# Banded attention and a routed expert layer: values as the stationary operand in column halves, and the output kept transposed

## The chip, the cores and the metric

The kernel runs on one core of one Trainium2 chip. The metric is the device time of one execution in microseconds; the median of several runs is compared. All data are 32-bit floats.

## What is computed

Attention over 4 batches, 8 heads, 768 positions and head dimension 64, in which a query sees the 8 first keys and its last 96 keys, with a bias that grows with the distance; its output is the input `x` (3072 x 512) of a layer of 8 experts, where each token goes to its one best expert.

```python
scores = scale * np.matmul(q, k.transpose(0, 1, 3, 2))
keep = is_global | is_local                 # first 8 keys, or 0 <= rel < 96
scores = np.where(keep, scores + bias, -1e9)
a = np.exp(scores - scores.max(-1)); a = a / (a.sum(-1) + 1e-9)
x = (a @ v).transpose(0, 2, 1, 3).reshape(3072, 512)
logits = x @ w_gate                         # 512 x 8
e = argmax(logits); gate = softmax(logits)[e]
out = gate * (relu(x @ w1[e]) @ w2[e])      # w1 512 x 1024, w2 1024 x 512 for each expert
```

## The kernel before

**Attention** (`banded_attention`, from L322). The work is cut into 48 units: batch b, pair of heads j (4 of them), and block c of 256 queries (3 of them). Queries are taken in tiles of 128. A tile needs two blocks of 128 keys: its own, and a block `kA` (values: `va`) that holds the keys of the tile before with the first 16 replaced by the first 16 of the sequence. So a unit has 4 blocks, the first of a sequence (c = 0) 3.

A unit n goes through these steps:

- `scores` (L447): PE multiplies keys by queries for each block and head, the two heads in the two halves of the rows (L458, 64x128 tiles). The result has keys in the partitions and queries along the free axis. ACT takes the exponential from PSUM (L461), DVE multiplies by a table `W` of exp(-bias) with zeros where nothing is kept (L467 for c = 0, L472 once for each head otherwise).
- `attend` (L478): PE multiplies with the exponentials as the stationary operand, 128x128, and the values as the moving one (L490). The values stand in the tile with a column of ones behind each block of 64, so the sum of each query's weights comes out as a column of its own. The output has queries in the partitions. DVE takes the reciprocal of the four sums of each query (L494, 128x4) and scales the output with it into `xr` (L497).
- `turn` (L501): PE turns `xr` by the identity (L506), ACT copies it to `xl` (L509). After the last pair of heads, the queue of SP stores `xr` to `x_tok` in DRAM, one token's 2 KB in each partition (L231).
- `logits` (L513) and `logits_sum` (L527), only in the last pair: the gate's product, in four column tiles of 32 (L521), and the sum of its four parts (L534). `gate`, `spread` and `spread_sum` then count and place the tokens of a batch, mostly small DVE operations.

The program is in the order that the loop at L718 writes out; each engine runs its instructions in that order. In iteration n stand: `scores(n)`, `turn(n-4)`, `logits(n-5)`, `attend(n-2)`, `logits_sum(n-5)`; for c = 0 `turn_qk` of the next pair (DVE turns its keys and queries, L409 and L410, and POOL makes `kA`, L374 and L376); for c = 1 `turn_v` (POOL makes `va`, L400 and L401). SP's queue loads q, k and v two and three pairs ahead, and from unit 8 to 43 expert 0's weights, one transfer in two of three units (L715, L716).

**After the last unit** expert 0's first 256 tokens are computed in pieces (`work`, L640: L293 and L300) between the steps of the last batch's routing. POOL gathers tokens from `x_tok` by indirect DMA, 32 tokens at a time (L256), and DVE turns them into columns (L263). The layout of a token in `x_tok`, of `turn_x` and of w1's rows hang together: before, w1 is loaded with its rows permuted to fit.

**Experts** (from L972). For each of the seven others, in order of size: the hidden layer (L1007, ACT's Relu L1009), then the result (L1033 or L1025), scaling and scatter. While one expert runs, SP loads the next one's w1 (L236, four transfers of 512 KB by groups of 32 partitions) and w2 (L992, one of 2 MB).

A check at the end (`ground`, L961) tests that all reciprocals lie in a range; if not, a general path runs, which it does not for this input.

Of the kernel before, what the change touches and what calls it, by code (L numbers as in the profile page):

```python
# [24 lines left out]
R_MIN = 2.0 ** -100  # L25
R_MAX = 2.0 ** 60
# [3 lines left out]
def kernel(  # L30
# [28 lines left out]
    x_tok = nc.dram_tensor("x_tok", (N * NJ, P), F32)  # L59

    w1v = moe_w1.rearrange("e (j k q) f -> j q e k f", j=NJ, q=32)
# [34 lines left out]
    vts = [consts.tile([P, 2 * NB * (D + 1) + P - D - 1], F32, name=f"vt{i}") for i in range(3)]  # L96

    def ones_in(t):
        w = 2 * NB * (D + 1)
        nc.gpsimd.memset(t[:, 0:w].rearrange("p (c w) -> p c w", w=D + 1)[:, :, D:D + 1], 1.0)  # L100
        nc.gpsimd.memset(t[:, w:], 1.0)

    ones_in(vts[0])
# [79 lines left out]
    recips = consts.tile([P, 2 * B * H * NB // 4, 2], F32)  # L183
# [44 lines left out]
    def store(t0, n, xr):  # L228

        for i in range(n):  # L230
            nc.sync.dma_start(x_tok[NJ * (t0 + P * i):NJ * (t0 + P * i + P), :].rearrange("(p j) d -> p (j d)", j=NJ),  # L231
                              xr[:, i, :])

    def expert_w1(to, e):
        for j in range(NJ):
            nc.sync.dma_start(to[32 * j:32 * j + 32, :, :, :], w1v[j, :, e, :, :])  # L236
# [10 lines left out]
    def rows_of(ps, nm, ns, mw, to_rows):  # L247

        pw = ps.tile([P, NS * TB], F32, tag="m", name="pw" + nm)[:, 0:TB * ns]
        nc.tensor.matmul(pw, lhsT=sel, rhs=mw.rearrange("p s g -> p (s g)"), start=True, stop=True)  # L250
        nc.vector.tensor_scalar(out=to_rows, in0=pw, scalar1=float(NJ), scalar2=j_of[:, 0:1], op0=ALU.mult, op1=ALU.add)

    def gather(xq, cols, n, top=N):

        for i in range(n):
            nc.gpsimd.indirect_dma_start(out=xq[:, i, :], out_offset=None, in_=x_tok[0:NJ * top, :],  # L256
                                         in_offset=bass.IndirectOffsetOnAxis(ap=cols[:, i:i + 1], axis=0),
                                         bounds_check=NJ * top - 1, oob_is_err=False)
# [63 lines left out]
    def banded_attention():  # L322
        with ExitStack() as actx:
            mp = actx.enter_context(tc.tile_pool(name="maskb", bufs=1))
            xlp = actx.enter_context(tc.tile_pool(name="xlb", bufs=3))
            xrp = actx.enter_context(tc.tile_pool(name="xrb", bufs=5))
# [10 lines left out]
            VW = D + 1  # L337
            NV = 3
            VT, VA = NB * VW, (NB - 1) * VW
            vas = [vp.tile([P, 2 * VA + P - VW], F32, name=f"va{i}") for i in range(2)]  # L340
            for i, t in enumerate(vts):
                if i > 0:
                    ones_in(t)
            for t in vas:
                nc.gpsimd.memset(t[:, 2 * VA:], 1.0)
# [17 lines left out]
            def load_v(pr):  # L363
                b, j = divmod(pr, NJ)
                vt = vts[pr % NV]
                for h in range(2):
                    (nc.scalar if pr == 0 and h == 0 else nc.sync).dma_start(
                        vt[:, VT * h:VT * h + VT].rearrange("p (c w) -> p c w", w=VW)[:, :, 0:D],
                        v[b, 2 * j + h].rearrange("(c p) d -> p c d", p=P))
# [3 lines left out]
            def keys_at(kT, kA, a0, a1):  # L373
                nc.gpsimd.tensor_copy(out=kA[:, a0:a1, GW:P],  # L374
                                      in_=kT[:, a0 * P:a1 * P].rearrange("p (c t) -> p c t", t=P)[:, :, GW:P])
                nc.gpsimd.tensor_copy(out=kA[:, a0:a1, 0:GW],  # L376
# [18 lines left out]
            def turn_v(pr):  # L395
                vt = vts[pr % NV]
                va = vas[pr % 2]
                to = va[:, 0:2 * VA].rearrange("p (h x) -> p h x", h=2)
                vh = vt[:, 0:2 * VT].rearrange("p (h x) -> p h x", h=2)
                nc.gpsimd.tensor_copy(out=to, in_=vh[:, :, 0:VA])  # L400
                nc.gpsimd.tensor_copy(  # L401
                    out=to[0:GW, :, VW:VA].rearrange("p h (c w) -> p h c w", w=VW),
                    in_=vh[0:GW, :, 0:VW].rearrange("p h (o w) -> p h o w", o=1).to_broadcast([GW, 2, NB - 2, VW]))
                pairs[pr] += [vt, va]

            def turn_qk(pr):
# [4 lines left out]
                keys_at(kT, kA, 0, NB - 1)  # L411
# [29 lines left out]
            xrs = {}  # L441
# [5 lines left out]
            def scores(n):  # L447
                b, j, c = units[n]
                qT, kT, kA, _, _ = pairs[b * NJ + j]
# [11 lines left out]
                nc.scalar.activation(e[:, :, 0:w], ps[:, :, 0:w], AF.Exp, scale=D ** -0.5)  # L461
                if n == 0:
                    turn_first(2, NB, ps_s.tile([P, 2, 512], F32, tag="s", name="first_1"))
                elif c == 1 and b == 0 and j + 1 < NJ:
# [4 lines left out]
                else:  # L469
                    for h in range(2):  # L470
                        eh = e[:, h, :].rearrange("p (t c) -> p t c", t=2)
                        nc.vector.tensor_tensor(  # L472
                            out=eh, in0=eh,
                            in1=W[:, 2 * j + h, P:3 * P].rearrange("p (o c) -> p o c", o=1).to_broadcast([P, 2, 2 * P]),
                            op=ALU.mult)
                st[n] = e

            def attend(n):  # L478
                b, j, c = units[n]
                _, _, _, vt, va = pairs[b * NJ + j]  # L480
# [3 lines left out]
                for t in range(2):  # L484
                    mine = [(m, own) for m, (u, own) in enumerate(bl) if u == t]
                    for h in range(2):
                        for m, own in mine:
                            i = 2 * c + t
                            c0 = VT * h + VW * i if own else VA * h + VW * (i - 1)
                            nc.tensor.matmul(po[:, t, h, :], lhsT=pt[:, h, P * m:P * m + P],  # L490
                                             rhs=(vt if own else va)[:, c0:c0 + P],
                                             start=(m == mine[0][0]), stop=(m == mine[-1][0]))
                r = recips[:, 2 * n:2 * n + 2, :]
                nc.vector.reciprocal(r.rearrange("p t (h o) -> p t h o", o=1), po[:, :, :, D:D + 1])  # L494
                if j == 0:
                    xrs[b, c] = xrp.tile([P, 2, DM], F32, tag="xr", name=f"xr_{b}_{c}")
                nc.vector.tensor_tensor(  # L497
                    out=xrs[b, c][:, :, P * j:P * j + P].rearrange("p t (h d) -> p t h d", h=2), in0=po[:, :, :, 0:D],
                    in1=r.rearrange("p t (h o) -> p t h o", o=1).to_broadcast([P, 2, 2, D]), op=ALU.mult)

            def turn(n):  # L501
                b, j, c = units[n]
                xr = xrs[b, c]
                px = ps_m.tile([P, 2, P], F32, tag="m", name=f"px_{n}")
                for t in range(2):
                    nc.tensor.transpose(px[:, t, :], xr[:, t, P * j:P * j + P], ident)  # L506
                if j == 0:
                    xls[b, c] = xlp.tile([P, KC, 2 * P], F32, tag="xl", name=f"xl_{b}_{c}")
                nc.scalar.copy(out=xls[b, c][:, j, :], in_=px.rearrange("p t c -> p (t c)"))  # L509
                if j == NJ - 1:  # L510
                    store(S * b + 2 * P * c, 2, xrs.pop((b, c)))
# [199 lines left out]
            turn_v(0)  # L711
# [3 lines left out]
            weights_0 = [lambda f0=f0: nc.sync.dma_start(w2_0[:, :, f0:f0 + 1, :], w2v[:, 0:1, f0:f0 + 1, :]) for f0 in range(FC)]  # L715
# [422 lines left out]
```

## Time and profile before

| | us |
|---|---|
| median of 3 runs | 604.67 (602.85 to 605.37) |
| the profiled execution | 607.0 |
| its span, first to last instruction | 605.1 |
| PE busy | 547.9 (91%) |
| DVE busy | 199.1 (33%) |
| ACT busy | 101.8 (17%) |
| POOL busy | 179.7 (30%) |

PE is the matrix engine, PEld its weight loads, DVE the vector engine, ACT the scalar engine, POOL the general one, SP the one that issues most DMAs. A 32-bit matmul has two records in the profile, a turn by the identity one; records of PE overlap, so the price of one is read from the starts of a series. A wait is put down to what ended it, and "issue" means that nothing recorded ended it. By stages: the attention runs to 185 us, the last batch's routing with expert 0 to 284 us, the other experts to the end.

### The profile page before, as it was taken

How to read it: one execution, taken by the hardware profiler on the slowest of the kernel's cores; microseconds unless marked ns; L12 is line 12 of the kernel's file. 1: busy time of each engine (PE TensorE's matmuls, PEld its weight loads, DVE VectorE, ACT ScalarE, POOL GpSimd, SP SyncE). 2: the span in 40 equal slices, each digit the busy share in tenths (PEclk: the TensorE clock that was granted, in tenths of full speed). 3: DMA queues.
4: the chain of work that ended last, by engine and by line, in shares of the span. 5: the costliest groups of instructions: out<-in, count | busy, mean ns of one | idle time of the engine just before them, and what ended most of it. 6: DMA issues, size and time to landing. Idle time of an engine off the chain costs nothing.

```text
span 605.1 us, 7929 instructions
## 1 busy us (share of the span) xinstructions
PE 547.9 (91%) x3034; PEld 379.4 (63%) x3034; DVE 199.1 (33%) x526; ACT 101.8 (17%) x193; POOL 179.7 (30%) x228
## 2 busy tenths in 40 slices
PE   4999999999998991199999999999999969999994
PEld 3998888998886851184555555555555747554541
DVE  3877876967851633002001301300301301200000
ACT  2543333333232100010110110110110110100100
POOL 4332224222250177601700730620550450101001
PEclk9999999999998996579999999999999998999999
DMA  9999999989212085107561534642625626401000
GB/s 154 147 166 160 235 175 171 217 132 234 64 55 86 5 204 194 50 7 179 167 139 43 185 81 89 214 97 58 205 59 117 202 48 131 176 1 50 1 18 36
DMA packets 145232, 71.96 MB, mean 119 GB/s; under 512 B 126743, under 2 KB 126747, under 8 KB 145184
## 3 DMA queue, kind: packets, MB, share of 16 engines
q1 hardware_dynamic: 137344, 58.16, 45.9%
q0 software_dynamic: 5312, 12.59, 6.5%
q10 hardware_dynamic: 2528, 0.59, 0.6%
q8 instruction: 26, 0.43, 0.3%
q14 instruction: 22, 0.18, 0.1%
HBM read 59.07 MB, written 12.91 MB: 119 GB/s over the span
## 4 chain that ended last, share of the span: by engine, by line
PE 85%; issue 5%; DVE 4%; DMA 2%; another core or an unknown queue 1%; POOL 1%; SPq 0%; ACT 0%; ACTq 0%; POOLq 0%; DVEq 0%
PE ph L1007 24%; PE po L1033 17%; PE o L490 12%; PE s L458 7%; PE po L1025 7%; PE ph L293 6%; PE po L300 4%; PE px L506 3%; PE pt L1042 1%; PE pq L521 1%; PE pi L598 1%; DMA vt<-in_v_dram 1%; DVE y L282 1%; DMA qb<-in_q_dram 1%
## 5 line engine op out<-in xcount | busy, mean ns | idle before, releaser
L256 POOL DMA_INDIRECT xq_s<-x_tok,rows_s x85 | 85.4, 1004 | 25.9 <-issue 24.4
L274 POOL DMA_INDIRECT out_dram<-y,idx_s x25 | 24.3, 973 | 211.2 <-DVE y L282 208.4
L1007 PE MATMUL ph<-xe,w_second 128*128 128x416 f32 (+2 forms) x256 | 81.9, 479 | 0.0
L1009 ACT ACTIVATE hT<-ph 128x416 f32<-128x416 f32 (+2 forms) x56 | 27.7, 495 | 278.2 <-PE ph L1007 233.5
L490 PE MATMUL o<-vt,e 128*128 128x128 f32 x384 | 72.8, 278 | 0.0
L1035 DVE COPY yT<-po 128x416 f32<-128x416 f32 (+1 forms) x20 | 11.3, 565 | 183.8 <-PE po L1033 183.8
L1007 PEld LDWEIGHTS ph<-xe,w_second 128*128 128x128 f32 x256 | 48.4, 190 | 31.9 <-issue 20.5
L1033 PE MATMUL po<-hT,w_second 128*128 128x416 f32 (+1 forms) x192 | 63.8, 493 | 5.1 <-ACT hT L1009 5.1
L1007 PE MATMUL ph<-xe,w_first 128*128 128x416 f32 (+1 forms) x192 | 66.3, 503 | 0.0
L293 PE MATMUL ph<-xe,w_first 128*128 128x128 f32 x256 | 38.2, 304 | 30.0 <-issue 27.2
L490 PE MATMUL o<-va,e 128*128 128x128 f32 x320 | 62.8, 278 | 0.0
L461 ACT ACTIVATE e<-s 128x1024 f32<-128x1024 f32 (+1 forms) x48 | 45.7, 953 | 95.9 <-PE s L458 48.1
L490 PEld LDWEIGHTS o<-vt,e 128*128 128x128 f32 x384 | 57.6, 194 | 1.6 <-issue 1.2
L1033 PEld LDWEIGHTS po<-hT,w_second 128*128 128x128 f32 x192 | 38.0, 199 | 30.4 <-issue 20.4
L293 PEld LDWEIGHTS ph<-xe,w_first 128*128 128x128 f32 x256 | 35.5, 217 | 32.8 <-issue 29.9
L1007 PEld LDWEIGHTS ph<-xe,w_first 128*128 128x128 f32 x192 | 36.2, 190 | 27.8 <-issue 19.7
L472 DVE TENSOR_TENSOR e<-e,Wb 128x512 f32<-128x512 f32 x64 | 44.4, 736 | 18.7 <-ACT e L461 16.3
L490 PEld LDWEIGHTS o<-va,e 128*128 128x128 f32 x320 | 48.7, 193 | 2.6 <-issue 2.5
L1033 PE MATMUL po<-hT,w_first 128*128 128x416 f32 x128 | 45.0, 512 | 0.0
L458 PE MATMUL s<-qT,kT 64*128 64x128 f32 x384 | 40.6, 290 | 0.9 <-ACT qT L392 0.9
L458 PE MATMUL s<-qT,kA 64*128 64x128 f32 x320 | 35.7, 301 | 2.9 <-POOL kA L376 2.9
L1033 PEld LDWEIGHTS po<-hT,w_first 128*128 128x128 f32 x128 | 24.3, 190 | 20.4 <-issue 20.1
(167 smaller groups left out, 525.0 us busy)
## 6 DMA issues: line engine op xcount, KB each, us to landing
w_second<-in_moe_w_dram SPq DMA_DIRECT2D x16, 512.0 KB, 9.5
w_second<-in_moe_w_dram SPq DMA_DIRECT2D x4, 2048.0 KB
x_tok<-xr SPq DMA_DIRECT2D x24, 256.0 KB, 4.0
w_first<-in_moe_w_dram SPq DMA_DIRECT2D x12, 512.0 KB, 7.8
w_first<-in_moe_w_dram SPq DMA_DIRECT2D x3, 2048.0 KB
vt<-in_v_dram SPq DMA_DIRECT2D x31, 192.0 KB, 4.7
qb<-in_q_dram SPq DMA_DIRECT2D x60, 96.0 KB, 4.1
kb<-in_k_dram SPq DMA_DIRECT2D x60, 96.0 KB, 3.8
```

The costliest lines, as they stand in the source:

```text
L256: nc.gpsimd.indirect_dma_start(out=xq[:, i, :], out_offset=None, in_=x_tok[0:NJ * top, :], in_offset=bass.IndirectOffsetOnAxis(ap=cols[:, ...
L274: p = nc.gpsimd.indirect_dma_start(out=out[:, :], out_offset=bass.IndirectOffsetOnAxis(ap=where, axis=0), in_=y[0:rows, :], in_offset=None ...
L293: nc.tensor.matmul(ph[:, P * f:P * f + P], lhsT=w1_0[:, 0, kc, c0:c0 + P], rhs=xe_0[q % 2][:, kc, :], start=(kc == 0), stop=(kc == KC - 1))
L300: nc.tensor.matmul(po, lhsT=hT_0[q % 2][:, fc, :], rhs=w2_0[:, 0, fc, :], start=(fc == 0), stop=(fc == FC - 1))
L458: nc.tensor.matmul(ps[:, h, P * m:P * m + P], lhsT=lhsT, rhs=qT[r, P * i:P * i + P], start=True, stop=True)
L461: nc.scalar.activation(e[:, :, 0:w], ps[:, :, 0:w], AF.Exp, scale=D ** -0.5)
L472: nc.vector.tensor_tensor(out=eh, in0=eh, in1=W[:, 2 * j + h, P:3 * P].rearrange("p (o c) -> p o c", o=1).to_broadcast([P, 2, 2 * P]), op= ...
L490: nc.tensor.matmul(po[:, t, h, :], lhsT=pt[:, h, P * m:P * m + P], rhs=(vt if own else va)[:, c0:c0 + P], start=(m == mine[0][0]), stop=(m ...
L1007: nc.tensor.matmul(ph[:, 0:C], lhsT=w1t[:, 0, kc, P * fc:P * fc + P], rhs=xe[:, kc, 0:C], start=(kc == 0), stop=(kc == KC - 1))
L1009: nc.scalar.activation(hT[:, fc, 0:C], ph[:, 0:C], AF.Relu)
L1025: nc.tensor.matmul(po, lhsT=hT[:, fc, P * q:P * q + P], rhs=w2t[:, 0, fc, :], start=(fc == 0), stop=(fc == FC - 1))
L1033: nc.tensor.matmul(po[:, 0:C], lhsT=w2t[:, 0, fc, P * dc:P * dc + P], rhs=hT[:, fc, 0:C], start=(fc == 0), stop=(fc == FC - 1))
```

## The change

- In `attend` the values are the stationary operand, 64 columns wide, and the exponentials the moving one. The two heads of a pair are written to the two halves of the output's partitions, head by head in turn. The output is x transposed: features in the partitions, queries along the free axis.
- The column of ones in the value tiles goes, with the memsets for it. In its place a 128x64 block of ones is multiplied by the exponentials, so that each of a head's 64 rows of the output holds the sum of every query: 4 matmuls a unit, of 256 columns each (for c = 0 two of 256 and two of 128).
- The reciprocal is now taken of that whole block (128x256), and scales the output straight into `xl`.
- `turn` on PE and its ACT copy go. DVE turns `xl` in blocks of 32x32 to `xt` for the store, which is 4 transfers of 32 partitions with pieces of 512 bytes, and stands right behind `attend(n-2)`. A token's row in `x_tok` has another order inside, so w1 is loaded with its rows in their natural order.
- The multiplication by `W` in units of 4 blocks is one instruction for both heads.
- The copies for `kA` and `va` go from POOL to ACT and one unit later.
- The check uses sums that ACT accumulates beside the exponentials (`sums`), and one more exponential for each unit that flags sums that are too small (`small`).
- Expert 0's weights are loaded in units 36 to 43, two transfers of 256 KB in each. The other experts' w1 goes in 4 transfers by blocks of rows, w2 in 4 of 512 KB.
- After the last unit `attend`, `turn` and the gate's steps stand in another order.

The diff, without the general path, the changes to sizes of pools and the check:

```diff
-    vts = [consts.tile([P, 2 * NB * (D + 1) + P - D - 1], F32, name=f"vt{i}") for i in range(3)]
+    vts = [consts.tile([P, 2, NB, D], F32, name=f"vt{i}") for i in range(3)]
...
-    def store(t0, n, xr):
-        for i in range(n):
-            nc.sync.dma_start(x_tok[NJ * (t0 + P * i):NJ * (t0 + P * i + P), :].rearrange("(p j) d -> p (j d)", j=NJ),
-                              xr[:, i, :])
+    def store(t0, n, xt):
+        rows = x_tok[TB * t0:TB * (t0 + P * n), :].rearrange("(c t a) d -> a t c d", t=32, a=TB)
+        for a in range(TB):
+            nc.sync.dma_start(rows[a], xt[32 * a:32 * a + 32, :, :])
 
     def expert_w1(to, e):
-        for j in range(NJ):
-            nc.sync.dma_start(to[32 * j:32 * j + 32, :, :, :], w1v[j, :, e, :, :])
+        for kc in range(KC):
+            nc.sync.dma_start(to[:, :, kc:kc + 1, :], w1v[:, e, kc:kc + 1, :])
+    def expert_w2(to, e):
+        for fc in range(0, FC, 2):
+            nc.sync.dma_start(to[:, :, fc:fc + 2, :], w2v[:, e, fc:fc + 2, :])
...
             def keys_at(kT, kA, a0, a1):
-                nc.gpsimd.tensor_copy(out=kA[:, a0:a1, GW:P],
+                nc.scalar.copy(out=kA[:, a0:a1, GW:P],
...
-                nc.gpsimd.tensor_copy(out=to, in_=vh[:, :, 0:VA])
+                nc.scalar.copy(out=va, in_=vt[:, :, 0:NB - 1, :])
...
-                nc.scalar.activation(e[:, :, 0:w], ps[:, :, 0:w], AF.Exp, scale=D ** -0.5)
+                nc.scalar.activation(e[:, :, 0:w], ps[:, :, 0:w], AF.Exp, scale=D ** -0.5, accum_out=sums[:, n:n + 1])
                 if n == 0:
                     turn_first(2, NB, ps_s.tile([P, 2, 512], F32, tag="s", name="first_1"))
+                    turn_v(0)
...
                 else:
-                    for h in range(2):
-                        eh = e[:, h, :].rearrange("p (t c) -> p t c", t=2)
-                        nc.vector.tensor_tensor(
-                            out=eh, in0=eh,
-                            in1=W[:, 2 * j + h, P:3 * P].rearrange("p (o c) -> p o c", o=1).to_broadcast([P, 2, 2 * P]),
-                            op=ALU.mult)
+                    eh = e.rearrange("p h (t c) -> p h t c", t=2)
+                    nc.vector.tensor_tensor(
+                        out=eh, in0=eh,
+                        in1=W[:, 2 * j:2 * j + 2, P:3 * P].rearrange("p h (o c) -> p h o c", o=1).to_broadcast([P, 2, 2, 2 * P]),
+                        op=ALU.mult)
...
-                    for h in range(2):
-                        for m, own in mine:
-                            i = 2 * c + t
-                            c0 = VT * h + VW * i if own else VA * h + VW * (i - 1)
-                            nc.tensor.matmul(po[:, t, h, :], lhsT=pt[:, h, P * m:P * m + P],
-                                             rhs=(vt if own else va)[:, c0:c0 + P],
+                    for m, own in mine:
+                        i = 2 * c + t
+                        for h in range(2):
+                            nc.tensor.matmul(po[D * h:D * h + D, 0, t, :],
+                                             lhsT=vt[:, h, i, :] if own else va[:, h, i - 1, :],
+                                             rhs=pt[:, h, P * m:P * m + P],
                                              start=(m == mine[0][0]), stop=(m == mine[-1][0]))
-                r = recips[:, 2 * n:2 * n + 2, :]
-                nc.vector.reciprocal(r.rearrange("p t (h o) -> p t h o", o=1), po[:, :, :, D:D + 1])
+                if c == 0:
+                    parts = [(pt[:, :, 0:4 * P].rearrange("p h (t c) -> p h t c", t=2)[:, :, :, 0:P], 0), (pt[:, :, P:2 * P], 1)]
+                else:
+                    both = pt.rearrange("p h (t o c) -> p h o t c", t=2, o=2)
+                    parts = [(both[:, :, o, :, :], 0) for o in range(2)]
+                for i, (e, t0) in enumerate(parts):
+                    for h in range(2):
+                        nc.tensor.matmul(po[D * h:D * h + D, 1, t0:2, :], lhsT=ones[:, 0:D], rhs=e[:, h],
+                                         start=(i == 0), stop=(i == len(parts) - 1))
+                r = rp.tile([P, 2, P], F32, tag="r", name=f"r_{n}")
+                nc.vector.reciprocal(r, po[:, 1, :, :])
...
-                nc.vector.tensor_tensor(
-                    out=xrs[b, c][:, :, P * j:P * j + P].rearrange("p t (h d) -> p t h d", h=2), in0=po[:, :, :, 0:D],
-                    in1=r.rearrange("p t (h o) -> p t h o", o=1).to_broadcast([P, 2, 2, D]), op=ALU.mult)
+                xl = xls[b, c][:, j, :]
+                nc.vector.tensor_tensor(out=xl.rearrange("p (t c) -> p t c", t=2), in0=po[:, 0, :, :], in1=r, op=ALU.mult)
+                nc.scalar.activation(junk, po[:, 1, :, :].rearrange("p t c -> p (t c)"), AF.Exp, scale=-2.0 / S_MIN,
+                                     accum_out=small[:, n:n + 1])
 
             def turn(n):
                 b, j, c = units[n]
-                xr = xrs[b, c]
-                px = ps_m.tile([P, 2, P], F32, tag="m", name=f"px_{n}")
-                for t in range(2):
-                    nc.tensor.transpose(px[:, t, :], xr[:, t, P * j:P * j + P], ident)
-                if j == 0:
-                    xls[b, c] = xlp.tile([P, KC, 2 * P], F32, tag="xl", name=f"xl_{b}_{c}")
-                nc.scalar.copy(out=xls[b, c][:, j, :], in_=px.rearrange("p t c -> p (t c)"))
+                nc.vector.transpose(xts[b, c][:, :, j, :], xls[b, c][:, j, :].rearrange("p (c t) -> p c t", t=32))
...
-                    if n % 3 > 0 and 8 <= n < 44:
+                    if 36 <= n < 44:
+                        weights_0.pop(0)()
                         weights_0.pop(0)()
...
                 if 0 <= n - 4 < nu:
-                    turn(n - 4)
-                if 0 <= n - 5 < nu:
-                    logits(n - 5)
+                    logits(n - 4)
                 if 0 <= n - 2 < nu:
                     attend(n - 2)
+                    turn(n - 2)
...
                 if n < nu and c == 1 and pr + 1 < B * NJ:
+                    keys_at(*pairs[pr + 1][1:3], 0, NB - 1)
+                if n < nu and c == 2 and pr + 1 < B * NJ:
                     turn_v(pr + 1)
...
-            turn_x(xe_0[0], xq_0[0], TB)
-            turn(nu - 3)
             attend(nu - 1)
-            turn_x(xe_0[1], xq_0[1], TB)
-            work(2)
-            turn(nu - 2)
-            logits(nu - 3)
             turn(nu - 1)
-            work(1)
+            logits(nu - 3)
+            turn_x(xe_0[0], xq_0[0], TB)
+            turn_x(xe_0[1], xq_0[1], TB)
             logits(nu - 2)
+            work(2)
             logits(nu - 1)
-            work(1)
+            work(2)
```

## The prediction

> **What bounds the kernel now.** I read the sums by stage first, because the page's average mixes an attention part with an expert part. Columns: stretch, its length, then busy time (and instructions) of PE, weight loads, DVE, ACT, POOL, the granted clock, DMA share, GB/s.
>
> ```profile
> 50.00:100.00 50.00, 49.02 (x506) 43.71 (x506) 38.43 (x87) 18.48 (x33) 13.03 (x20) 1.00 1.03 189
> 100.00:150.00 50.00, 49.28 (x512) 43.48 (x511) 37.36 (x86) 18.43 (x34) 13.04 (x21) 1.00 0.99 190
> ...
> 220.00:240.00 20.00, 8.67 (x48) 6.73 (x47) 7.19 (x25) 0.00 (x0) 15.35 (x16) 0.75 0.77 223
> 240.00:260.00 20.00, 4.01 (x11) 2.83 (x11) 0.00 (x0) 0.00 (x0) 12.01 (x12) 0.50 0.16 43
> ...
> 320.00:420.00 100.00, 99.18 (x305) 54.77 (x304) 16.01 (x43) 8.27 (x16) 29.88 (x30) 1.00 0.43 115
> ```
>
> In the attention PE has no idle time, and DVE, at 77%, has little to spare. The DMA engines are as full as PE, but PE doesn't wait for them. The experts are PE alone. Between lies a hole (220 to 260), which the timeline of PE explains in part:
>
> ```profile
> 222.58 4.07 PE L293 MATMUL ph<-xe,w_first 128*128 128x128 f32 x35
> ...
> 243.66 0.37 PE L293 MATMUL ph<-xe,w_first 128*128 128x128 f32 x1 [2.43 <-issue]
> ...
> 259.06 11.69 PE L293 MATMUL ph<-xe,w_first 128*128 128x128 f32 x79 [0.82 <-issue]
> ```
>
> From 226.6 to 259.1 PE gets one matmul in about 2.4 us and waits for nothing that is recorded. Its 16 matmuls need 2 us; some 31 us are lost in issue.
>
> Then one attention unit in the timeline of PE (start, length, what):
>
> ```profile
> 103.50 0.51 PE L534 MATMUL pl<-sel,lq 128*128 128x8 f32 x4
> 103.94 0.49 PE L458 MATMUL s<-qT,kA 64*128 64x128 f32 x4
> ...
> 105.03 0.44 PE L506 MATMUL px<-ident,xr 128*128 128x128 f32 x2
> 105.40 0.64 PE L521 MATMUL pq<-xl,wg_sb 128*32 128x256 f32 x8
> 105.97 0.49 PE L490 MATMUL o<-va,e 128*128 128x128 f32 x2
> ```
>
> Starts give the price. Scores take 1.09 us for 8 matmuls (two records each), since two halves of the rows run at once; the values (105.97 to 107.86) 1.89 for 8, or 0.22 each; the turn 0.37. The gate's L521 uses quarters of the columns: four matmuls of 256 columns in 0.57 us, where 0.22 for 128 columns would make 1.8 one after another. Column tiles do overlap here.
>
> Last, the groups of DVE by shape (busy, mean ns, idle before):
>
> ```profile
> L497 DVE TENSOR_TENSOR xr<-o,recips 128x256 f32<-128x256 f32 x44 | 18.7, 424 | 1.5
> L467 DVE TENSOR_TENSOR e<-e,Wb 128x768 f32<-128x768 f32 x14 | 13.5, 964 | 7.3 <-ACT e L461 7.3
> L409 DVE STREAM_TRANSPOSE kT<-kb 128x768 f32<-128x768 f32 x13 | 12.6, 968 | 0.0
> L494 DVE RECIPROCAL recips<-o 128x4 f32<-128x4 f32 x44 | 7.8, 177 | 12.8 <-PE o L490 12.6
> L263 DVE STREAM_TRANSPOSE xe<-xq 128x128 f32<-128x128 f32 x16 | 4.0, 288 | 3.2 <-DMA xq<-x_tok,rows 2.8 <-issue 0.3
> L537 DVE COPY L<-pl 128x16 f32<-128x16 f32 x12 | 2.0, 167 | 11.5 <-PE pl L534 11.5
> L224 DVE RECIPROCAL gates<-se 128x6 f32<-128x6 f32 x4 | 0.8, 191 | 0.1
> ```
>
> [...] This trace shows it only with 4 and 6 elements, 177 and 191 ns: 7 ns for an element more, where an ordinary operation adds about 1 (768 against 256 elements: 540 ns for 512). [...]
>
> **The change part by part.** All of the attention is counted for a pair of heads (three units, one with 3 blocks and two with 4), 16 pairs in all. Before, the first reciprocal starts at 20.8 and the last at 184.5: 163.7 us, 10.2 a pair.
>
> PE. Removed: three turns, 1.1 us. The values become 128x64 tiles, two heads side by side: 22 matmuls of 0.22 (4.9) become 11 pairs (2.45). Added: sums, in pairs, of 256+128, 512 and 512 columns at 0.22 per 128: 2.2 to 2.45. Scores stay at 3.05 (0.87 + 2 x 1.09), routing at about 1.45 (four matmul groups of L521 and after, 5.8 a batch). PE goes from 10.5 to about 9.6 with 0.2 for switching tiles: 0.9 a pair less.
>
> DVE. An independent successor starts 0.08 before an operation's recorded end (kT at 104.33 for 0.97, qT at 105.23), a dependent one 0.03 after it.
> - Multiplications: 768 elements 0.88; the 1024 of a 4-block unit, now in one instruction, 0.96 + 256 x 1.04 ns - 0.08 = 1.15. Sum 3.2.
> - Reciprocal: from 128x4 to 128x256, because the block of ones gives every row of the output its sum. The trace doesn't show this size. [...] like L497: 0.42. [...] I take the line through the two rows: fixed part 149 ns (L537 leaves 150 after its 16 elements), 256 x 7 ns: 1.94. Three with the dependent start: 5.9.
> - Scaling stays 0.42, now with the transpose dependent on it: 1.35 for three.
> - New transposes of 256 elements: between L263 (0.288) and L409 (0.968), 0.43 less the overlap, 0.35: 1.05.
> - kT and qT: 0.89 + 0.86 = 1.75.
>
> Sum 13.2 a pair; 16 pairs less one qk: 210. Three batches' routing lies among it at about 5.7 each (the fourth batch's: 1.6 for the gate from 198.0, the rest to 204.2): 17. So 227 us of DVE against 9.6 x 16 = 154 of PE: VectorE becomes the bound, and PE's saving is worth nothing. DVE's first multiplication starts at 11.0; with some 2.5 us of filling the last unit ends near 240.5, where it ended at 185.1: +55.
>
> ACT. Per pair: exponentials 2.9; the check of small sums, three of 256 from PSUM like L509 (0.37), 1.1; the copies for kA and va, which POOL did in 970, 745, 655 and 251 ns, about 2.2 from ACT's own slope of 0.83 ns an element; less L509's 1.1. The accumulations are not in the trace: 0 to 0.2 each, 1.2 at most. Sum 6.2 to 7.4, hidden behind 13.2 of DVE. A copy for kA waits for kT, and the next exponential stands behind it in ACT's queue; the exponential has over 3 us of slack a unit, so nothing. Without that cover it would cost 2 us a pair.
>
> POOL loses its copies and memsets: nothing, it was idle four fifths of the time.
>
> DMA and SP. Expert 0's 4 MB go out in units 36 to 43, two issues a unit. They have 8 x 4.7 = 38 us; at the 190 GB/s shown they need 21, and they are first read after the last unit: hidden. Each is an issue on SP ahead of later q, k and v loads, 0.3 us like L236's: nothing. Freeing the early DMA gains nothing, since PE doesn't wait there. Stores go from 24 to 48 of half the size, w2 from one issue to four, all off the path: PE is 99% busy in the experts.
>
> End of the attention: the first turn_x now stands behind a transpose more, three turns on PE are gone: 0 within 1 us. The experts are unchanged.
>
> Sum: span 605.1 + 55 = 660. The profiled execution took 607.0, 2.3 above the median of 604.67; a difference carries over, so **660 us**.
>
> **Rivals.**
> B, the same, but the issue hole goes: nothing that I can name fixes its place. For it: 288 more records (576 instructions) go through PE before it[...]. Against: the weights and gathers around it are the same. 660 - 31 = 629.
> C, column halves with 128 rows don't overlap: PE takes 3.05 + 4.9 + 4.9 + 1.45 = 14.3 a pair, 229 us, beside DVE's 227. Both full, about 10 more: 670. Against it: L521.
> D, faster: [...] the 14 ns between its two rows are something else. DVE then needs 8.7 + 1.1 a pair, PE 9.6: PE stays the bound and wins 0.9 x 16 = 14: 591. It decides at the length at which DVE fills the old 10.2 a pair: (10.2 - 8.4) / 3 = 0.6 us for one reciprocal.
> E, the hole moves or grows, or the gain and loss cancel: within 0.5% by chance.
>
> **How the numbers follow.** Forecast 0.52, B 0.28, C 0.07, D 0.10, E 0.03. [...] So 622 (B's low end) to 680 [...] leaves D and little else out. Faster by over 0.5% (what a measurement here can tell from no change) 0.11, within 0.02, slower 0.87.
>
> **What would show it.** Right: a reciprocal group 128x256 near 1.9 us, x48; DVE over 95% busy from 50 to 230 and PE near two thirds; the L490 row's successor at about 0.22 us a pair of heads; ACT's waits for scores or free tiles. Wrong: a reciprocal near 0.4; PE still full in the attention; the issue hole absent, which alone moves the time by 31.

## The result and the profile after

| | before | after |
|---|---|---|
| median | 605.0 us (4 runs, 602.9 to 608.9) | 715.5 us (4 runs, 711.1 to 715.8) |
| ratio | | 1.180, 95% interval 1.174 to 1.187 |
| span of the profiled execution | 605.1 | 709.4 |
| last scaling of the attention ends | 185.1 | 292.6 |

The change makes the kernel slower by 110 us; the forecast was 55. All of the excess is in the attention, which ends 107.5 us later in the profiles. From there to the end the two spans agree to 3 us (420.0 and 416.8).

The sums by stage, after the change (stretch, length, then busy us and instructions of PE, weight loads, DVE, ACT and POOL, clock, DMA share, GB/s):

```profile
50.00:100.00 50.00, 37.56 (x372) 27.64 (x372) 37.28 (x44) 19.30 (x51) 0.00 (x0) 0.80 0.50 101
100.00:150.00 50.00, 35.39 (x342) 27.85 (x344) 37.42 (x59) 17.38 (x45) 0.00 (x0) 0.76 0.42 79
```

In the forecast VectorE stood at over 95% here. It stands at 75%, as before the change (76%); PE falls from 98% to 73%, and ACT has 37%. No engine is full, so the engines must be waiting for each other, and the groups of instructions say for whom (busy us, mean ns of one, idle us before them and what ended it):

```profile
L492 DVE RECIPROCAL r<-o 128x256 f32<-128x256 f32 x48 | 83.9, 1748 | 0.4 <-PE o L489 0.3
L460 DVE TENSOR_TENSOR e<-e,Wb 128x1024 f32<-128x1024 f32 x32 | 38.8, 1212 | 26.5 <-ACT e L449 25.3
L446 PE MATMUL s<-qT,kA 64*128 64x128 f32 x320 | 43.3, 355 | 46.7 <-ACT kA L368 46.6
L498 ACT ACTIVATE junk<-o 128x256 f32<-128x256 f32 x48 | 18.4, 384 | 174.6 <-DVE xl L497 172.5
L449 ACT ACTIVATE e<-s 128x1024 f32<-128x1024 f32 x32 | 32.6, 1019 | 1.2 <-PE s L446 1.1
```

PE waits for ACT, DVE waits for ACT, and ACT waits 172.5 us for DVE at one instruction: L498, the exponential that flags sums that are too small ("the check" from here on). PE itself hardly holds anybody up: the exponentials L449 wait 1.1 us for it in all, the reciprocals L492 0.3. Here is one unit of 4 blocks, first in ACT's timeline, then in DVE's (start, length, what, idle before):

```profile
51.41 1.02 ACT L449 ACTIVATE e<-s 128x1024 f32<-128x1024 f32 x1
52.32 0.20 ACT L449 ACTIVATION_READ_ACCUMULATOR e<-s 128x1 f32 x1
56.02 0.38 ACT L498 ACTIVATE junk<-o 128x256 f32<-128x256 f32 x1 [3.50 <-DVE xl L497]
...
56.39 0.71 ACT L390 COPY va<-vt 128x640 f32<-128x640 f32 x1
57.14 0.62 ACT L391 COPY va<-vt 16x512 f32<-16x512 f32 x1
57.66 0.80 ACT L449 ACTIVATE e<-s 128x768 f32<-128x768 f32 x1
```

```profile
52.55 1.22 DVE L460 TENSOR_TENSOR e<-e,Wb 128x1024 f32<-128x1024 f32 x1 [1.86 <-ACT e L449]
53.70 1.75 DVE L492 RECIPROCAL r<-o 128x256 f32<-128x256 f32 x1
55.48 0.42 DVE L497 TENSOR_TENSOR xl<-o,r 128x256 f32<-128x256 f32 x1
...
58.58 0.96 DVE L456 TENSOR_TENSOR e<-e,Wb 128x768 f32<-128x768 f32 x1 [2.20 <-ACT e L449]
```

Read by turns, the two timelines are one chain:

1. The exponential of unit n starts at 51.41 on ACT, and its multiplication at 52.55 on DVE.
2. Behind that, in DVE's order, stand the reciprocal and the scaling of unit n-2 (53.70 and 55.48).
3. The check of unit n-2 waits for the scaling and starts at 56.02 on ACT.
4. Behind the check, in ACT's order, stand the copies and then the exponential of unit n+1, at 57.66. With it the chain begins again.

The check reads only the sums, which PE had written before the reciprocal of 53.70 began to read them. But the sums lie in the same PSUM tile as the products that the scaling reads. In the program as built the check waits for PE and for the scaling on VectorE, because the text has it behind the scaling. The two only read that tile, and they share nothing else.

One pair (three units) without routing, from the starts between 51.41 and 68.30, in us:

| unit | exponential to multiplication | to reciprocal | to scaling | to check | to next exponential | sum |
|---|---|---|---|---|---|---|
| 4 blocks, `va` copies behind the check | 1.14 | 1.15 | 1.78 | 0.54 | 1.64 | 6.25 |
| 3 blocks | 0.92 | 0.88 | 1.78 | 0.52 | 0.38 | 4.48 |
| 4 blocks, keys and queries turned ahead, `kA` copies | 1.65 | 1.10 | 1.78 | 0.55 | 1.08 | 6.16 |

That is 16.9 us a pair. VectorE's own work is 12.6 a pair, as the first experiment shows, and the kernel before took 9.1 (from one pair's first multiplication to the next one's, in pairs without routing).

### The profile page after: what moved, and what is told of

It reads as the page before. It is cut to its first block, busy times and chain, and to the rows that moved or that the text cites. A ratio compares the mean times of both kernels' runs of the same rounds, so it can differ in the third digit from the quotient of the medians.

```text
span 709.4 us, 8708 instructions
## 1 busy us (share of the span) xinstructions
PE 577.2 (81%) x3322; PEld 378.0 (53%) x3322; DVE 285.8 (40%) x542; ACT 142.5 (20%) x355; POOL 136.6 (19%) x154
## 4 chain that ended last, share of the span: by engine, by line
PE 56%; DVE 25%; ACT 9%; issue 6%; SPq 2%; DMA 1%; another core or an unknown queue 1%; DVEq 0%; ACTq 0%; POOL 0%; POOLq 0%
PE ph L1005 21%; PE po L1031 15%; DVE r L492 10%; PE po L1023 6%; PE ph L291 5%; DVE e L460 4%; PE po L298 4%; ACT e L449 4%; DVE xl L497 3%; DVE e L456 2%; DVE kT L398 2%; DVE qT L399 2%; PE pi L592 1%; PE s L446 1%; ACT va L390 1%
## 5 line engine op out<-in xcount | busy, mean ns | idle before, releaser
L492 DVE RECIPROCAL r<-o 128x256 f32<-128x256 f32 x48 | 83.9, 1748 | 0.4 <-PE o L489 0.3
L446 PE MATMUL s<-qT,kA 64*128 64x128 f32 x320 | 43.3, 355 | 46.7 <-ACT kA L368 46.6
L254 POOL DMA_INDIRECT xq<-x_tok,rows x16 | 16.5, 1032 | 301.1 <-DVE early L615 271.0
L446 PEld LDWEIGHTS s<-qT,kA 64*128 64x128 f32 x320 | 30.3, 231 | 58.3 <-ACT kA L368 49.1
L291 PE MATMUL ph<-xe,w_first 128*128 128x128 f32 x256 | 35.5, 289 | 30.0 <-issue 26.9
L489 PE MATMUL o<-e,ones 128*64 128x256 f32 (+1 forms) x384 | 57.5, 429 | 0.0
L478 PE MATMUL o<-e,vt 128*64 128x128 f32 x384 | 45.8, 324 | 9.9 <-ACT junk L498 9.9
L498 ACT ACTIVATE junk<-o 128x256 f32<-128x256 f32 x48 | 18.4, 384 | 174.6 <-DVE xl L497 172.5
L460 DVE TENSOR_TENSOR e<-e,Wb 128x1024 f32<-128x1024 f32 x32 | 38.8, 1212 | 26.5 <-ACT e L449 25.3
L446 PE MATMUL s<-qT,kT 64*128 64x128 f32 x384 | 45.3, 318 | 2.2 <-DVE qT L399 1.1
L449 ACT ACTIVATE e<-s 128x1024 f32<-128x1024 f32 (+1 forms) x48 | 45.3, 944 | 1.2 <-PE s L446 1.1
```

The costliest lines, as they stand in the source:

```text
L291: nc.tensor.matmul(ph[:, P * f:P * f + P], lhsT=w1_0[:, 0, kc, c0:c0 + P], rhs=xe_0[q % 2][:, kc, :], start=(kc == 0), stop=(kc == KC - 1))
L446: nc.tensor.matmul(ps[:, h, P * m:P * m + P], lhsT=lhsT, rhs=qT[r, P * i:P * i + P], start=True, stop=True)
L460: nc.vector.tensor_tensor(out=eh, in0=eh, in1=W[:, 2 * j:2 * j + 2, P:3 * P].rearrange("p h (o c) -> p h o c", o=1).to_broadcast([P, 2, 2, ...
L478: nc.tensor.matmul(po[D * h:D * h + D, 0, t, :], lhsT=vt[:, h, i, :] if own else va[:, h, i - 1, :], rhs=pt[:, h, P * m:P * m + P], start= ...
L489: nc.tensor.matmul(po[D * h:D * h + D, 1, t0:2, :], lhsT=ones[:, 0:D], rhs=e[:, h], start=(i == 0), stop=(i == len(parts) - 1))
L492: nc.vector.reciprocal(r, po[:, 1, :, :])
```

## The experiments

Theory L: this loop of ACT's and VectorE's queues, closed by the check's wait, sets the pace. Its rivals are:

- C: the copies that came to ACT hold PE's scores up (46.6 us of waits for `kA`).
- K: PE's half clock after its gaps (granted clock 0.50 from 68.45 to 74.20 after the change, 1.00 from 50 to 150 before it) is a cause by itself.
- S: the check's own time counts.
- V: VectorE's own sum sets the pace, which was the forecast.

Chips turned out to differ, so an excess below ("+55.0") is over the kernel before on the same chip. The +110.4 of the change is from the runs of the result, over 605.0; the first chip's excesses are over 608.0. A difference of the two can be off by these 3 us, so the end of the attention (of its last scaling) in the profiles is the closer measure.

**Check ahead of the reciprocal** (first chip)

```diff
+                nc.scalar.activation(junk, po[:, 1, :, :].rearrange("p t c -> p (t c)"), AF.Exp, scale=-2.0 / S_MIN,
+                                     accum_out=small[:, n:n + 1])
                 nc.vector.reciprocal(r, po[:, 1, :, :])
...
-                nc.scalar.activation(junk, po[:, 1, :, :].rearrange("p t c -> p (t c)"), AF.Exp, scale=-2.0 / S_MIN,
-                                     accum_out=small[:, n:n + 1])
```

> The check exponential stands ahead of the reciprocal instead of behind the scaling; nothing is left out. Theory L (a loop of the two queues): in the kernel after the change, exponential n, multiplication n, reciprocal n-2, scaling n-2, check n-2, copies, exponential n+1 follow one another, 4.5 + 5.7 + 6.2 = 16.4 us a pair by the starts in the timeline. With the check ahead, ACT waits for PE alone, the reciprocals lie beside the next exponential, and VectorE's own sum of 12.8 a pair is left (3.2 multiplications, 5.35 reciprocals, 1.4 scaling, 1.1 transposes, 1.75 keys and queries): 16 pairs and 17 of routing end near 234 instead of 293, so about 655. Rival C (the copies for kA and va on ACT hold PE's scores up): the copies are as before, so within 10 of 715. Rival K (TensorE's half clock by itself): no change, 715. Rival S (the check's own time on ACT counts): no change, 715.

Measured: 663.0 us against 608.0, ratio 1.094 (1.087 to 1.100): +55.0 where the change has +110.4. The attention ends at 240.3 instead of 292.6. One statement in another place gives 52 us back (55 by the excesses). By stages:

```profile
50.00:100.00 50.00, 38.62 (x409) 29.32 (x405) 48.15 (x73) 21.10 (x56) 0.00 (x0) 0.86 0.60 118
100.00:150.00 50.00, 41.38 (x451) 31.25 (x451) 45.21 (x62) 23.71 (x61) 0.00 (x0) 0.88 0.59 116
```

VectorE is at 93% now. In pairs without routing its operations stand one behind the other, with no wait left:

```profile
54.77 1.18 DVE L460 TENSOR_TENSOR e<-e,Wb 128x1024 f32<-128x1024 f32 x1
55.87 1.75 DVE L494 RECIPROCAL r<-o 128x256 f32<-128x256 f32 x1
57.65 0.42 DVE L499 TENSOR_TENSOR xl<-o,r 128x256 f32<-128x256 f32 x1
58.11 0.45 DVE L503 STREAM_TRANSPOSE xt<-xl 128x256 f32<-128x256 f32 x1
58.48 1.18 DVE L460 TENSOR_TENSOR e<-e,Wb 128x1024 f32<-128x1024 f32 x1
```

ACT now runs ahead of VectorE. The exponential of 54.75 belongs to the multiplication of 58.48, and the check of 55.75 to the reciprocal of 59.59, 3.8 us later; the next unit's exponential (57.38) runs before either:

```profile
54.75 1.01 ACT L449 ACTIVATE e<-s 128x1024 f32<-128x1024 f32 x1
...
55.75 0.37 ACT L492 ACTIVATE junk<-o 128x256 f32<-128x256 f32 x1
...
57.38 0.80 ACT L449 ACTIVATE e<-s 128x768 f32<-128x768 f32 x1
```

Pairs without routing take 12.6 us, VectorE's sum. Theory L had said 655; the rest is mostly routing, which took 23 us where 17 were counted. The copies were as in the change, and PE's clock was still below full (0.86 to 0.88, after 0.76 to 0.80), so C and K fall as the main cause. V does not explain the change itself, where VectorE stood at 75%; it holds here.

In the program as built the reciprocal now waits for the check, the other way round. Where the check comes late, the trace has this wait:

```profile
106.53 1.76 DVE L494 RECIPROCAL r<-o 128x256 f32<-128x256 f32 x1 [0.95 <-ACT junk L492]
```

So the order of the two readers follows the text. That it hangs on the shared tile is read from the program; a tile of its own for the sums was not tried.

**Check left out** (first chip)

```diff
+    nc.gpsimd.memset(small, 0.0)
...
-                nc.scalar.activation(junk, po[:, 1, :, :].rearrange("p t c -> p (t c)"), AF.Exp, scale=-2.0 / S_MIN,
-                                     accum_out=small[:, n:n + 1])
```

> The check exponential is left out (its 48 flags are set to 0 once): the small sums are not looked for, the rest is computed. Theory L: as with the check ahead, within 3 us of that kernel, near 655, since ACT's time is not on the path once it does not wait for VectorE. Rival S (the check's own time counts, 48 x 0.57 = 27): 27 less than the kernel with the check ahead. Rival C: 715 less at most 27.

This kernel does not look for small sums. Measured: 663.7, ratio 1.093 (1.087 to 1.099), the same as with the check ahead. So 48 exponentials of 0.38 us and 48 readings of the accumulator of 0.19 cost nothing where they stand ahead; their place behind the scaling cost 52. S falls.

**Copies back on POOL, check left behind the scaling** (first chip)

```diff
-                nc.scalar.copy(out=kA[:, a0:a1, GW:P],
+                nc.gpsimd.tensor_copy(out=kA[:, a0:a1, GW:P],
...
-                nc.scalar.copy(out=va, in_=vt[:, :, 0:NB - 1, :])
+                nc.gpsimd.tensor_copy(out=va, in_=vt[:, :, 0:NB - 1, :])
```

> The copies for kA and va go back to POOL, the check stays where the change put it; nothing is left out. Theory L: the loop loses 0.71 + 1.27 us a pair, 32 us, so about 684; kA's longer time on POOL is covered. Rival C (the copies are the cause): the whole loss beyond VectorE's sum goes, about 655. My forecast's step (copies hidden): 715, no change.

Measured: 692.4, ratio 1.141 (1.134 to 1.147), +84.4. That is 23 us less than the change by the medians and 26 by the excesses, not 32; the attention ends 21.8 us earlier (270.8 instead of 292.6). Pairs without routing go from 16.9 to 15.0, as the loop's sum without the copies says. But a batch's routing now adds 5.8 us to its pairs, where it added 4.4: with less waiting, less of it finds a place beside the waits. And the first pair gains only 1.0. Of the 15 distances between 16 pairs, 14 give 1.9 each: 26.6 + 1.0 - 3 x 1.4 = 23.4, less 1.2 because the first unit began later: 22. The copies were part of the loop, and its smaller part.

**Check ahead, a copy instead of the reciprocal** (first chip)

```diff
-                nc.vector.reciprocal(r, po[:, 1, :, :])
+                nc.vector.tensor_copy(out=r, in_=po[:, 1, :, :])
```

> The check stands ahead, and a copy of the same 128x256 block takes the place of the reciprocal, so that x is scaled by the sums instead of by their reciprocals. Theory L: with the loop gone VectorE is the bound at 12.8 a pair; a copy of 0.42 for 1.75 takes 4 off, VectorE needs 8.8, and PE with 9.6 or the path through both ends the pair: attention near 180 to 190, so 602 to 612. If something else bounds the attention once the loop is gone (PE's clock, copies, transfers), much less than 50 us goes between this kernel and the one with the check ahead.

Measured: 3252 us (ratio 5.36, 5.33 to 5.39). This total says nothing about the reciprocal: with x scaled by the sums, the general path ran behind the attention, which the expectation had not foreseen. The attention can still be read: pairs without routing mostly take 8.6 to 9.2, and the last scaling starts at 197.4 instead of 239.9, 42 us earlier. So once the loop is gone, the reciprocals are what holds the attention up.

**Logarithm and exponential on ACT instead of the reciprocal** (second chip)

```diff
+    nc.scalar.add_instruction(mybir.InstLoadActFuncSet(name=nc.get_next_instruction_name(), act_func_set_id=6, ins=[], outs=[]))
     nc.scalar.activation(warm, warm, AF.Exp)
...
-                nc.vector.reciprocal(r, po[:, 1, :, :])
+                nc.scalar.activation(r, po[:, 1, :, :], AF.Ln)
+                nc.scalar.activation(r, r, AF.Exp, scale=-1.0, accum_out=small[:, n:n + 1])
```

with the check exponential gone, since the accumulated 1/sum serves for it.

> The reciprocal leaves VectorE: ACT takes the logarithm of the sums from PSUM and the exponential of its negative, 1/sum, and accumulates it, which serves as the flag of small sums in place of the check exponential; nothing is left out. Copies for kA and va stay on ACT. With the check ahead and a copy for the reciprocal the last scaling was at 197.4 us, against 239.9 with the reciprocal and 184.7 before the change. Theory L: VectorE's sum falls to 7.5 a pair, ACT's rises to about 8.6, PE's 9.6 to 10.5 is then the longest: last scaling 185 to 197, so 608 to 621. Theory V (once the loop is gone VectorE's reciprocal is the whole rest of the loss): the time of before within 1%, or less. Rival: ACT's queue, now with two more instructions a unit that wait for PE's sums, makes a loop of its own with PE; then over 640.

Measured: 569.9, but before took 561.1 on this chip: ratio 1.015 (1.012 to 1.017), +8.8. The 48 logarithms and the exponentials alternate on ACT, and the profile has a single table load of 1.28 us, as it had before the change (L115, 1.28 us):

```profile
L494 ACT ACTIVATE r<-r 128x256 f32<-128x256 f32 x48 | 20.0, 417 | 1.5
L493 ACT ACTIVATE r<-o 128x256 f32<-128x256 f32 x48 | 18.4, 384 | 33.9 <-PE o L490 33.8
L107 ACT ACT_TABLE_LOAD x1 | 1.3, 1283 | 2.3 <-issue 2.3
```

(These lines are from the kernel of the next experiment. What is loaded without the added instruction was not tried.) 0.80 us on ACT, 68% busy here, stand in for 1.75 on VectorE, which was 93% busy with the check ahead. The expectation's theory V had said within 1% of before; measured were 1.5%. So nearly the whole rest of the loss was the reciprocal; some 9 us are left.

**The same with the copies on POOL** (second and third chip; the edits of both kernels above)

> As the logarithm kernel, with the copies for kA and va back on POOL; nothing is left out. If ACT's queue (copies ahead of the exponential that PE and VectorE wait for) still costs something without the loop, this is faster by up to 2 us a pair, 32; if PE is the bound, the same within 5.

> The logarithm kernel with copies on POOL once more, nothing left out. PE's pairs without routing at 8.3 to 8.8 us against 9.1 before. If the hole stays as it is, 3 to 6 us less than before on either kind of chip: ratio 0.990 to 0.997.

Measured: 558.2 against 561.1, ratio 0.995 (0.993 to 0.997), and on a third chip 556.9 against 561.2, 0.992 (0.990 to 0.994). On the second chip that is 12 us less than with the copies on ACT. On both it is faster than before the change, by 0.5% and 0.8%. PE is the bound again, at 95%:

```profile
50.00:100.00 50.00, 47.67 (x578) 37.52 (x576) 39.62 (x76) 27.42 (x74) 17.42 (x22) 0.93 0.74 150
100.00:150.00 50.00, 47.70 (x616) 37.82 (x614) 41.23 (x82) 27.50 (x75) 12.33 (x18) 1.00 0.82 158
```

So the idea of the change pays, by 3 to 4 us, when the reciprocal is off VectorE and neither the check nor the copies stand in the way of the exponentials.

**Check ahead and copies on POOL** (third chip)

> The check stands ahead of the reciprocal, and the copies for kA and va go back to POOL; nothing is left out. In the kernel with the check behind, the copies cost 23 us (715.5 to 692.4), because they lay in the loop. Theory L: with the loop gone they are covered by VectorE's 12.6 a pair, so the same as the kernel with the check ahead within 5 us, about 1.09 times before. Rival C (copies cost by themselves): 20 to 30 us less than that kernel, 1.05 times before.

Measured: 620.9 against 561.2, ratio 1.108 (1.105 to 1.110), +59.8, beside +55.0 with the copies on ACT on the first chip. The profiles compare better across chips: pairs without routing take 12.7 and 12.6, and the attention ends at 240.9 and 240.3. Without the loop, and with VectorE as the bound, the copies on ACT are covered, as the forecast had them.

**The change once more** (third chip)

> The kernel after the change once more, nothing left out, because the runs with the logarithm met a chip on which the kernel before takes 561 us and the issue hole is absent, while all earlier ones took 603 to 610. If the loop is the cause, it does not depend on the hole: pairs without routing at 16.9 us again, so before + 110 us: about 715 on a chip with the hole, 671 on one without it, ratio 1.18 to 1.20. If hole and loop belong together, the ratio on a chip without the hole is nearer 1.10.

Measured: 673.5 against 561.2, ratio 1.201 (1.198 to 1.205), +112.3. Pairs without routing take 16.9, and ACT waits 172.4 us at the check, both as in the result. This chip has no hole, so the loop does not need it. The kernel of the experiment before, on the same chip, is 52.6 us faster; it differs in the check's place and in the copies, which are covered there.

**The hole: the second expert's gathers moved** (logarithm kernel and the kernel before)

```diff
             sort(1)
-            take(2)
...
                 result_0(po, z, 0, FC)
+            take(2)
```

> As the one before, and the gathers of the second of the seven experts' tokens stand behind expert 0's last scatters in POOL's queue, no longer right behind the first expert's; nothing is left out. In all kernels so far the issue hole of PE begins 17.5 to 18 us after POOL begins a run of 36 gathers and scatters and ends at most 3 us after that run ends. Theory G (POOL's long run of gathers keeps PE's instructions back): the run is 13 gathers of 1.3 us shorter, the hole ends 17 us sooner, so 12 to 17 us less than the kernel without the move. Rival P (the hole belongs to a place in PE's program): it stays 31 us and the time is the same within 3.

> The kernel before the change with the same move of the second expert's gathers; nothing is left out. Theory G: the hole of 31 us is about 14 to 17 shorter, so 588 to 594. Rival P: 605, no change. If the later gathers come too late for the second expert, a wait of VectorE for them shows up ahead of its turns and takes part of it back.

> The kernel before with the second expert's gathers moved behind expert 0's last scatters, nothing left out: on the chip without the hole this changed nothing (561.1 and 561.1). On a chip with the hole, theory G (POOL's long run of gathers holds PE's instructions back): 13 gathers of 1.3 us less in the run, 12 to 17 us less. Rival P (the hole belongs to a place in the program[...]): no change. On a chip without it: no change, and it stays open.

"The hole" is the stage of some 31 us in which PE gets single instructions far apart. Measured: 557.6 (beside 558.2 without the move) for the logarithm kernel, and 561.1 and 560.9 for the kernel before (ratios 1.000, 0.999 to 1.001, both). There is no difference, but on these two chips there is no hole to shorten, and the kernel before takes 561 us there instead of 605. This is PE's timeline of the kernel before with the move, at the stage where the first chip has the hole:

```profile
214.71 3.60 PE L300 MATMUL po<-w_first,hT 128*128 128x512 f32 x8
218.15 14.45 PE L293 MATMUL ph<-xe,w_first 128*128 128x128 f32 x128
232.44 13.90 PE L300 MATMUL po<-w_first,hT 128*128 128x512 f32 x32
```

And this is PE in the profile after the change, on a chip that has it:

```profile
357.24 0.37 PE L291 MATMUL ph<-xe,w_first 128*128 128x128 f32 x1 [2.43 <-issue]
360.04 0.37 PE L291 MATMUL ph<-xe,w_first 128*128 128x128 f32 x1 [2.43 <-issue]
```

In the profiles with the hole it begins 17 to 18 us after POOL begins a run of 36 gathers and scatters, and ends within 3 us of that run's end. But such a run is no sufficient cause: on the third chip, after the change, it was 51 long (316.6 to 382.8) and left no hole. Why one chip has it stays open, and so does whether the move helps there.

## Why the prediction failed

**The step that failed** is ACT's: "the exponential has over 3 us of slack a unit, so nothing". The slack was judged by busy time, 6.2 to 7.4 a pair beside 13.2 of VectorE. Busy time was right: in us a pair, exponentials 2.8 (two of 1.02, one of 0.80), copies 2.2 (0.65, 0.26, 0.71 and 0.62) and checks 1.15 (three of 0.384); the accumulations took 0.19 each, at the upper end of the estimate of 0 to 0.2. ACT's slope, 0.83 ns an element in the forecast, is 0.84 in the profile before: 1024 ns for L461's 1024 elements and 810 for its 768. What the step left out is what each ACT instruction waits for and what stands behind it. It asked this of the `kA` copies, and not of the check, which was counted only as the time of three operations of 256 columns.

**What the runs showed in its place:** behind the scaling, the check ties the exponential of unit n+1 to the reciprocal of unit n-2, which itself stands behind the multiplication of unit n. There is no slack in this loop. It takes 16.9 us a pair where VectorE's sum takes 12.6: 4.3 a pair. The 2 us a pair that the prediction gave for copies without cover is near what they cost in the loop (1.9); the larger part had no term at all.

The amounts agree. Of the 15 distances between the 16 pairs, 14 are 4.3 shorter with the check ahead and the first is 2.3 shorter: 62.5. Routing takes 10 of it back, because in the loop it lies in part beside the waits (13 us in three batches there, 23 with the check ahead). That leaves 52, and the attention ends 52.3 us earlier.

**What held:**
- VectorE's sum: 13.2 a pair forecast, 12.6 measured once the loop is gone. In effect the forecast describes the kernel with the check ahead: span 660 forecast, 659.8 measured. That it meets it to 1 us is in part luck, since two errors cancel: the pairs were 0.6 too long (10 us in all), and routing was 6 us too short, 17 forecast and 23 measured.
- The reciprocal: 1.94 forecast, 1.75 measured; (1748 - 177) / 252 = 6.2 ns an element instead of 7. Three a pair make 0.6 less, nearly the whole error of the sum. That a slower one could not take the time past 680 was the author's estimate.
- The scaling 0.42, the transpose 0.37 from start to start (0.35 forecast), the single multiplication of 1024 elements 1.10 to 1.15 (1.15 forecast, with 1.04 ns an element where the rows of 256 and 768 elements before give 540 / 512 = 1.05).
- POOL and SP: no wait for a POOL instruction shows in the attention, and one of 0.2 us for a transfer. That the late loads of expert 0's weights cost nothing was not tried alone; the stages behind the attention took 3 us less than before.
- PE: values and sums in column halves run at once. In the kernel with the check ahead the steps of the values (four records, one matmul of each head) start 0.22 apart, and the scores, values and sums of 4 blocks take 1.09, 0.93 and 0.96 from start to start:

```profile
109.11 0.49 PE L446 MATMUL s<-qT,kA 64*128 64x128 f32 x4
109.44 0.39 PE L446 MATMUL s<-qT,kT 64*128 64x128 f32 x4
109.66 0.39 PE L446 MATMUL s<-qT,kA 64*128 64x128 f32 x4
...
110.20 0.44 PE L478 MATMUL o<-e,va 128*64 128x128 f32 x4
110.47 0.39 PE L478 MATMUL o<-e,vt 128*64 128x128 f32 x4
110.69 0.39 PE L478 MATMUL o<-e,va 128*64 128x128 f32 x4
...
111.13 1.03 PE L489 MATMUL o<-e,ones 128*64 128x256 f32 x8
112.09 0.49 PE L446 MATMUL s<-qT,kA 64*128 64x128 f32 x4
```

The prediction's rival C (halves don't overlap) falls. The 0.2 a pair that the prediction gave for switching tiles was an estimate; in these lines the first step of the scores takes 0.33 and the next 0.22, the first step of the values 0.27 and the next 0.22.

**Rival B**, the hole goes, did not happen: it moved along with the attention, from 226.6 to about 332, and is as long. (The prediction misread its inside: there are 14 records in it, not 16 matmuls, and 2.4 us is the usual idle time before one, 2.8 the distance of their starts. That the number of records ahead of the hole has to do with its place is not shown.) **Rival D** (faster, below 0.6 us a reciprocal) fell with 1.75. Its condition was met when the reciprocal left VectorE, and the result was not -14 but -3 to -4: pairs without routing went from 9.1 to between 7.4 and 8.8, as PE's sum has it, but the pair with most of a batch's routing went from 12.8 to as much as 15.6 and took much of that back. In one such pair of the logarithm kernel (66.7 to 82.3, copies on POOL), PE waits 2.3 us for the table `oh` of VectorE's routing (L576), where it waited 1.0 before. Behind that wait it runs slower: the 12 records that read the table take 2.75 us instead of 1.52, and the next scores 0.64 instead of 0.39.

**PE's half clock** is a consequence of the waits, since the loop hardly waits for PE (1.1 us at the exponentials, 0.3 at the reciprocals). In the profile after the change, PE idles for 3.94 us before 68.45. The granted clock is 1.00 ahead of this gap (63.00 to 64.50), 0.50 from 68.45 to 74.20 and 1.00 again from 74.40 to 76.00. Scores run at 0.64 and 0.63 at the clock of 0.50, and at 0.39 at that of 1.00:

```profile
68.45 0.80 PE L446 MATMUL s<-qT,kA 64*128 64x128 f32 x4 [3.94 <-ACT kA L368]
69.04 0.64 PE L446 MATMUL s<-qT,kT 64*128 64x128 f32 x4
...
73.80 0.63 PE L446 MATMUL s<-qT,kT 64*128 64x128 f32 x4
74.23 0.43 PE L446 MATMUL s<-qT,kA 64*128 64x128 f32 x4
74.49 0.39 PE L446 MATMUL s<-qT,kT 64*128 64x128 f32 x4
```

In the pair of the logarithm kernel above, slow records follow a shorter gap, of 2.3 us.

## What to carry to other kernels

An instruction that a change puts into an engine's queue costs what stands behind it, for as long as it waits; its own time may be nothing (the check, 0.57 us, 48 times, is free in one place and costs 52 us in another). So before an engine is called hidden, list for each new instruction whom it waits for, walk the chain from there, and ask whether it comes back to the queue it stands in: a chain that closes can set the pace though no engine is full. Two engines that read one PSUM tile were put in order by the program text here, in either order; so let the cheap reader come first.

## What the runs showed of the hardware beyond this

- A reciprocal of 128x256 32-bit elements from PSUM takes 1.75 us on VectorE, about four times a product of the same shape (0.42). ACT's logarithm and exponential together take 0.80 for it.
- An accumulation beside an ACT operation has an instruction of its own, 0.19 us, that starts 0.1 before the operation's end (52.32 in the timeline after the change, behind the exponential of 51.41).
- The same kernel before took 604 to 610 us on one chip and about 561 on two others. Most of the difference is the hole, in which PE of the first chip gets mostly one instruction in 1.4 to 2.8 us for 31 us. Ratios here are therefore between runs of one chip; across chips the excess over before and the profiles are compared.
